# A mirrored spectrum formed by accumulating DMAs instead of extra matmuls, in a gated state-space and expert-mix kernel

## The chip, the cores and the metric

One NeuronCore of a Trainium2 chip. The time is device microseconds of one execution; the median of three runs counts. Engines: PE (matrix multiply, with PEld loading its weights), DVE (vector), ACT (scalar), POOL (GpSimd) and SP (which mostly issues DMAs).

## The reference, cut to what matters

```python
x = A_u                                              # (1, 2048, 512) bf16
g = sigmoid((x * gate_w).sum(-1, keepdims=True))
# a: K[d, l] = Re sum_n C[d,n] * exp(dt[d] * A[d,n] * l) * dt[d] * B[d,n],   l = 0..2047, n = 0..127
#    y = causal convolution of x with K along l (FFT of length 4096), a = bf16(y) + x * Dskip
# b: r = x @ w_r; the two tokens with the largest r go through a gated MLP (512 -> 1792 -> 512);
#    its result times sigmoid(r) is added to those two rows of x
return g * a + (1 - g) * b
```

## The kernel before, in words

All data lies in one SBUF tensor `AR`, cut by hand into buffers with fixed offsets; PSUM is four tensors `ps` of two banks. The convolution goes through transforms written as matmuls. The 2048 tokens are two blocks (`blk`) of 1024, the 512 channels two halves (`h`) of 256.

- `tab1` and `tab2` build the powers of the kernel's poles for one half (exponentials and sines on ACT, products on DVE; `trig` makes the sines), `kgen` multiplies the two tables on PE, `kspec` turns the result into the spectrum `KK[h]` with the constants `KP` (loaded by SP).
- `routing` transposes U into `XT`, makes the gates and the router logits, picks the two tokens and runs their MLP with the weights `WG`, `WU`, `WD`. The finished rows come by an indirect DMA on POOL (L854), and U is then read again from the output (`reload`).
- `forward(blk)` is the transform of the input U with the constants `F[ft]`, four frequency tiles `ft`. A frequency and its mirror share their work: with E the part of the even tokens and O that of the odd ones, the one is E + O (`pm` 0), the other E - O (`pm` 1). Before the change each tile issues 16 matmuls of 512 columns for E + O (two parts, real and imaginary, eight steps each), an eviction into X, 8 more matmuls with `UO`, which is the odd tokens times -2, on top of the same PSUM banks, and a second eviction (L881 are the matmuls, L466 the evictions, L472 the scaling into UO).
- `products` multiplies X with KK on DVE (L451; its big instructions are 128x4096) and forms the sum and the difference of the two mirrored halves in place in X. Its temporaries are `pqa`, `pqb`, `pqc`.
- `inverse` transforms back on PE (L1028) on top of PSUM banks that ACT has filled with the other branch (L462, 256 columns), evicts times the gate into U (L1036), and DMAs the output.

Every operation is recorded in program order with its reads and writes, and its number is its place there. Nothing is scheduled on the chip: the string `ORDER` lists the operations by number, three base-36 digits each, and each engine takes its own in that order. Operations with two forms, such as `EV` (L466, copy), `SCL` (L472, scale) or an angle addition (L650), carry both, and the digit of `SECOND` at the operation's number chooses between ACT and DVE. `PLACES` gives each PSUM bank or temporary its place. Waits are worked out from the reads and writes. DMA issues are operations too, on SP, ACT or POOL, and wait in their queue like any other. The shared line of a helper covers many operations: L451 is every `TT` on DVE, L466 every `EV`, L475 every issue of a DMA by `DMA`.

`X` holds 32 KB per partition, ordered by half, block, part and `pm`; `XT` and `WD` lie for a time where the second block of X will be.

Of the kernel before, what the change touches and what calls it, by code (L numbers as in the profile page):

```python
# [241 lines left out]
MUL1 = [(16, 4, 24, 4, 1), (20, 0, 24, 4, 1), (28, 15, 24, 4, -1)]  # L242
# [11 lines left out]
ACC = ((1, 0),)  # L254
CPE = (0,)
# [97 lines left out]
def small_mats():  # L353
# [15 lines left out]
POOLS = {"pqa": 2, "pqb": 2, "pqc": 4}  # L369
ORDER = (  # L370
    "01l00200k01501600500000u00100400700o00p00q00601j01g00t00w00v01001201h01d01901e01100900r01a00300s01701x00801v00d00g00h02701t00x01r01y01400y01300c00f00z"
    "00l02500b00i01800a02801c01s01w01p01q00n00e02302601u02101z05n02402002201b03w04002901f06i01o01n03x08d03y06h08f05m02a02j03v02k01i04102l08e01m02b06j02m03z"
    "02n02c02o00m03702p05302q02r04202d02s06k02t06l04302u03404b05402v02w04506m04405h02x04802y04902z04a04c03003804603103204p04d05503904q04f03304704g04e04i04j"
    "03c03503l03d04h05g04k05o04m04r06p03g04l04n04u06q05q03h04o06n04s03i04w06o04t05604v06w03k00j03p03o06v06y06x03m03j06r08r01k06s04y03a04z03605p05707003n06z"
    "05805b05006t05i05907107204x07307405a08i08q05r05c06u07607505108g08j08h07807705205k08s05j05z07a03q08k07905d07h07b08t05l03b08u03r05e07c05s06003s07e07f03t"
    "07g07i08l06107j07d06606508n08v06306708x08o08y05f08m08w06206806909l06a08p08z07l07k07n09009206409u09m07m07o07q07z07r09107p09409309509n07s09o09r09609p07w"
    "07u09t07t07x09q09s09z0970980800a006b06c09c0990a20a102e09a09b09d08a06d09v09w05u05t09e0a30a408909g06f09h0a60a509x09f0a70a809i0aa06e0a905v07v05w07y05x03e"
    "06g08308403f09y09k0ac0ab08109j0ad0ae0820ag08b0af08508808c03u0aq0ar0ay0860aj0as0at05y0az0ao0ap0au0ah0ai0al0ak0am0an0b00b10av0aw0ax0ch0b80b90bc0be0870bb"
    "0bi0bf02f0ba0bd0bh0ci0cj0bg0bk0c40c10bj02g0ck0bz0cl0bl0bn0bm0b50bw02h0bo0b20b60c00b30b40br0c30bx0c20by0bp0bs0bq0bt0b70ct0bu02i0c50c60c70c90e80e70e90c8"
    "0cm0cu0bv0cn0co0cr0cv0d30cs0ea0cy0cb0eg0ez0cp0d40cw0cx0cz0eb0eh0cq0d10em0ep0d00e60d50ec0d20d60f40ed0e50d70f00f50ee0f10f20f60eq0df0er0ca0cc0dg0ei0es0f9"  # L380
    "0ef0f30ce0cd0f70f80dh0dn0fw0d80fx0dc0db0d90fy0ej0cf0dl0g40da0ek0en0et0fa0cg0dp0dv0dd0eu0di0dj0dk0do0dy0fz0de0eo0fs0g00dz0e00dq0dm0ds0g10g50dr0ft0fb0fc"
    "0g20fu0fv0el0fd0fe0fg0gc0gp0ff0dw0gm0dx0gd0g60g30go0gn0ge0gq0gt0gr0dt0fh0fi0fk0fj0ey0gf0g90gx0gu0ev0gg0ga0gs0e40e30du0gb0e20ew0e10g70gi0gw0gh0ex0gv0gz"
    "0fl0gk0fm0fo0fn0gl0gy0h80h00fp0h40fq0h10fr0h20g80gj0h50h30h60h70hh0hg0hc0h90ha0hd0he0hi0hf0hb0hj"
)
SECOND = (
    "000000000000000000000000000000000000100000000000000000000000000010101000101010100000000100000000000000000000000000100010000000000000000000000001000101"
    "001110010100010010000010010010000100000000000000000000000000000000000000000000000000000000001010000010000000000001000000000000000000000000000000000000"
    "000000000101000000010100011010000010011010000000100010001000001000000000000000000000000000000000000000000000000000000000000000000000000000000000000000"
    "000000000000000000000000000000000000000000000000000000000000000000000000000000000000000000000000000000000000000000000000000000000000001000000000000000"
    "00000000000000010000001100100000"  # L390
)
PLACES = (
    "2004756176414666666067000110100264042421011602064766100101111004004220204264646600000004406600706142350206200227354163"
# [4 lines left out]
def bass_gated_mix__ssm_conv_s4__moe_arch_mod__prompt_kernel(nc, A_u, A_A_re, A_A_im, A_B_re, A_B_im, A_C_re, A_C_im, A_log_dt, A_Dskip,  # L398
# [22 lines left out]
    with ExitStack() as es:  # L421
# [42 lines left out]
        def EV(o, a, rd, wr, **k):  # L464
            n = nel(o)
            return P.op((ACT, DVE), (lambda h: h.activation(out=o, in_=a, func=ACTF.Copy), lambda h: h.tensor_copy(o, a)), rd, wr,  # L466
                        cost=(0.185 + n * 0.833e-3, 0.16 + n * (1.04e-3 if a.dtype == F32 else 0.52e-3)), **k)
        def AFF(o, a, c, d, rd, wr):
            return P.op((DVE, ACT), (lambda h: h.tensor_scalar(out=o, in0=a, scalar1=c, scalar2=d, op0=ALU.mult, op1=ALU.add), lambda h: h.activation(out=o, in_=a, func=ACTF.Copy, scale=c, bias=d)), rd, wr, cost=(0.18, 0.2))
# [24 lines left out]
        UO = B("uo", oF + 16 * KB, 4 * KB)  # L494
# [3 lines left out]
        XB = [[B("x%d%d" % (h_, k_), oX + (16 * h_ + 8 * k_) * KB, 8 * KB) for k_ in range(2)] for h_ in range(2)]  # L498
# [17 lines left out]
        XT = [B("xt%d" % i, oX + (16 * (i // 2) + 8 + 4 * (i % 2)) * KB, 4 * KB) for i in range(4)]  # L516
        WD = [B("wd%d" % i, oX + (16 * i + 8) * KB, 8 * KB) for i in range(2)]
# [5 lines left out]
        PQR = [[B("pqa", oTI[0], 8 * KB), B("pqb", oTI[0] + 8 * KB, 8 * KB)], [B("pqc", oI, 16 * KB)] * 2]  # L523
# [60 lines left out]
        for r in range(2):  # L584
            P.op(PE, scaled(at(AL, r * 512), 0, True, 1 + r), [(PRM, 0), DG], [(AL, r)], cost=0.5 * (1 + r))
        P.op(PE, scaled(at(tb_), 1, True), [(PRM, 1), DG], [tb_], cost=0.5)
# [7 lines left out]
        for i in range(2):  # L594
            P.op(PE, ptr(i), [(PRM, 2 + i), CBI], [(cc, i)], cost=0.5)
        for i in range(2):
            P.op(PE, scaled(at(bd, i * 512), 4 + i, True), [(PRM, 4 + i), DG], [(bd, i)], cost=0.5)
# [56 lines left out]
        def tab1(h, ts):  # L654
            tr = TP[h][1]
            e = lambda *ss: [(tr, ("e", s)) for s in ss]
            for o, a, b, n, d in MUL1:
                src = [a + i * d for i in range(n)]
                assert all(T1[o + i] == T1[x] + T1[b] for i, x in enumerate(src))
                v = lambda s0, st: tr(0, 128, 4 * s0, (128, 64), (st, n), (1, 4))  # L660
                TT(v(o, 4), v(a, 4 * d), v(b, 0), ALU.mult, e(b, *src), e(*range(o, o + n)))
# [32 lines left out]
        def tab2(h, ts):  # L694
# [11 lines left out]
            TT(pair(q2(0), q2(1)), pair(sq(eb, 0), sq(di, 0)), pair(sq(eb, 0), sq(di, 0)), MUL, ed, [(qa, 0), (qa, 1)])  # L706
# [32 lines left out]
        def routing():  # L739
            for q in range(8):  # L740
# [8 lines left out]
                EV(XT[0](0, 128, q * 256, (8 * KB, 2), (L, 2), (1, 256)), bb(0, 128, 0, (512, 2), (256, 2), (1, 256)), [bb], [(XT[i], q) for i in range(4)])  # L749
# [118 lines left out]
        def forward(blk):  # L868
                SCL(UO(0, 128, 0, (1, 4 * D)), U(0, 128, (blk * 8 + 1) * D, (2 * D, 4), (1, D)), -2.0, uk(*range(blk * 8 + 1, blk * 8 + 8, 2)), [UO])
                for ft in range(4):  # L870
                    pb = psum(2, full=True)
                    for pm in range(2):
                        for part in range(2):
                            def fw(h, blk=blk, ft=ft, pm=pm, pb=pb, part=part):
                                last = None
                                o = pb(0, 128, part * 512, (1, 512))
                                for par in range(pm, 2):
                                    for st in range(4):
                                        w = F[ft](0, 128, ((par * 4 + st) * 2 + part) * 128, (1, 128))
                                        x = UO(0, 128, st * D, (1, D)) if pm else U(0, 128, (blk * 8 + st * 2 + par) * D, (1, D))  # L880
                                        last = h.matmul(o, w, x, start=(pm + par + st == 0), stop=(par == 1 and st == 3), skip_group_check=(pm == 1))  # L881
                                return last
                            P.op(PE, fw, [F[ft]] + ([UO] if pm else uk(*range(blk * 8, blk * 8 + 8))), [(pb, part)], cost=(8 - 4 * pm) * 0.2157)
                        EV(X(0, 128, blk * 4096 + ft // 2 * 1024 + pm * 512 + ft % 2 * 256, (2048, 2), (8192, 2), (1, 256)), pb(0, 128, 0, (512, 2), (256, 2), (1, 256)),
                           [pb], [xk(hh, blk, part, pm, ft) for hh in range(2) for part in range(2)])
# [75 lines left out]
        def products(h, qds, blks):  # L961
# [3 lines left out]
            xo = lambda blk, part, pm: h * 8192 + blk * 4096 + part * 2048 + pm * 512 + q0  # L965
# [7 lines left out]
            tmp = lambda k: place("pq%s" % ("ab"[k] if h == 0 else "c"), PQR[h][k], (oTI[0] + 8 * k * KB, oI)[h], 8 * W, n=2)  # L973
            qk = lambda b, *ks: [(b, k) for k in ks]
            for blk in blks:
                p = tmp(0)
                TT(o2(p), x2(blk), k2(0), MUL, kx(blk) + kk(0, 0) + kk(0, 1), qk(p, 0, 1, 2, 3))
                if blk == 1:
                    t = tmp(1)
# [15 lines left out]
                else:  # L995
                    if blk == 1:
                        TT(vall(p), vall(p), vall(t), ADD, qk(t, 0, 1, 2, 3), qk(p, 0, 1, 2, 3))
                    TT(u(0), u(0), u(3), SUB, qk(p, 3), qk(p, 0))
                    TT(u(1), u(1), u(2), ADD, qk(p, 2), qk(p, 1))
                for parts in (((0,), (1,)) if last(h, blk, qds[-1]) else ((0, 1),)):  # L1000
                    n, p0 = len(parts), parts[0]
                    y = lambda pm: p(0, 128, (2 * p0 + pm) * W, (2 * W, n), (1, W))
                    for pm, op in ((0, ADD), (1, SUB)):
                        TT(X(0, 128, xo(blk, p0, pm), (2048, n), (1, W)), y(0), y(1), op, qk(p, *parts), [xk(h, blk, part, pm, ft) for part in parts for ft in fts])
        def inverse(h):
            for blk in (1, 0):
# [11 lines left out]
                for q in range(2):  # L1018
                    for t2 in range(2):
                        for par in range(2):  # L1020
                            pb = bufs[t2, par]
                            for cs in (((0, 2), (1, 3)) if last(h, blk, q) else ((0, 1, 2, 3),)):
                                def iv(hh, blk=blk, par=par, t2=t2, pb=pb, q=q, cs=cs):
                                    r = None
                                    for e in range(2):
                                        for c in cs:
                                            part, ft = c % 2, 2 * q + c // 2
                                            r = hh.matmul(pb(0, 128, e * 256, (1, 256)), G(0, 128, ((par * 2 + part) * 4 + ft) * 512 + (2 * t2 + e) * 128, (1, 128)),  # L1028
                                                          X(0, 128, h * 8192 + blk * 4096 + part * 2048 + ft // 2 * 1024 + par * 512 + ft % 2 * 256, (1, 256)), start=False, stop=(q == 1 and e == 1 and c == 3), skip_group_check=True)
# [4 lines left out]
                            for e, tb in enumerate(tbs(t2, par)):  # L1034
# [82 lines left out]
```

## Time and profile before

| what | value |
|---|---|
| runs | 153.46, 152.22, 152.40 us, median 152.40 |
| the profiled execution | 153.67 us in all, span 151.9 us |
| granted TensorE clock | 0.988 |
| busy: PE, DVE, ACT, POOL | 140.4, 140.1, 128.3, 6.7 us |
| forward matmuls L881 | 192, 44.9 us busy |
| DMA | 22.01 MB, mean 145 GB/s |

The span runs from the first to the last instruction of the profiled execution. Busy time counts instructions that overlap once; a row's mean is one instruction's own duration, which for DVE and ACT is about 0.1 us longer than its step to the next. In a timeline row the first number is the start and the second the time to the end of the last of its instructions. Windows show busy time per engine in a stretch, with the number of instructions.

### The profile page before, as it was taken

To read this page: it belongs to the slowest core of one execution; us is meant where nothing else is said; L and a number is where in the kernel's file an instruction comes from. 1 tells how busy PE (TensorE), PEld (TensorE's weight loads), DVE (VectorE), ACT (ScalarE), POOL (GpSimd) and SP (SyncE) were. 2 spreads that over 40 slices of the span, in tenths; PEclk is the share of its full clock that TensorE was granted. 3 is DMA by queue.
4 is the path that set the end of the run, shared out by engine and by line. 5 is a ranking of instruction groups with operands and counts; after the bars stand their busy time and mean duration, and the time that the engine had idled before them with its cause. 6 is when DMAs were issued, how large, how long until landed. Compare 5 with 4: busy or idle time off the path is not lost.

```text
span 151.9 us, 3913 instructions
## 1 busy us (share of the span) xinstructions
PE 140.4 (92%) x1677; PEld 101.9 (67%) x1677; DVE 140.1 (92%) x201; ACT 128.3 (84%) x215; POOL 6.7 (4%) x13
## 2 busy tenths in 40 slices
PE   1977969999999999979999999999999999999990
PEld 1866633665446447975436889987888678888980
DVE  0489999999999999988999999999999999999972
ACT  3589999999999979998996568486999899899831
POOL 3000000000000000000540000010000000000000
PEclk9999999996899999999999999999999999999999
DMA  4899999939000001600029920007920000202166
GB/s 117 287 368 413 406 405 394 349 104 539 17 0 4 0 0 27 254 4 0 0 63 296 403 76 0 4 4 218 404 76 0 0 2 4 71 0 69 39 198 182
DMA packets 12435, 22.01 MB, mean 145 GB/s; under 512 B 1111, under 2 KB 8034, under 8 KB 12258
## 3 DMA queue, kind: packets, MB, share of 16 engines
q1 hardware_dynamic: 11410, 21.11, 39.4%
q10 hardware_dynamic: 976, 0.66, 1.5%
q8 instruction: 13, 0.21, 0.6%
q14 instruction: 4, 0.03, 0.1%
q0 software_dynamic: 32, 0.00, 0.1%
HBM read 19.66 MB, written 4.20 MB: 157 GB/s over the span
## 4 chain that ended last, share of the span: by engine, by line
PE 76%; DVE 13%; ACT 6%; issue 1%; DMA 1%; SPq 0%; DVEq 0%
PE ps L881 22%; PE ps L1028 18%; PE ps L954 12%; PE ps L899 8%; DVE AR L451 5%; ACT AR L466 3%; DVE AR L466 3%; PE ps L912 3%; PE ps L990 2%; PE ps L829 2%; PE ps L580 2%; ACT AR L462 2%; DMA AR<-c_bf 1%; PE ps L591 1%; DVE AR L472 1%
## 5 line engine op out<-in xcount | busy, mean ns | idle before, releaser
L451 DVE TENSOR_TENSOR AR<-AR 128x1024 bf16<-128x1024 bf16 (+8 forms) x132 | 118.5, 949 | 5.5 <-ACT AR L462 3.7
L466 ACT ACTIVATE AR<-ps 128x1024 bf16<-128x1024 f32 (+10 forms) x60 | 49.6, 861 | 11.3 <-PE ps L954 3.9
L881 PE MATMUL ps<-AR 128*128 128x512 bf16 x192 | 44.9, 389 | 0.0
L881 PEld LDWEIGHTS ps<-AR 128*128 128x128 bf16 x192 | 18.5, 100 | 21.8 <-issue 1.6
L1028 PE MATMUL ps<-AR 128*128 128x256 bf16 x256 | 29.3, 273 | 0.0
L1028 PEld LDWEIGHTS ps<-AR 128*128 128x128 bf16 x256 | 24.9, 98 | 3.5 <-DVE AR L451 0.3
L954 PE MATMUL ps<-AR 128*128 128x256 bf16 x160 | 19.0, 273 | 0.0
L899 PE MATMUL ps<-AR 128*128 128x84 bf16 (+1 forms) x512 | 18.0, 196 | 0.9 <-ACT AR L462 0.9
L899 PEld LDWEIGHTS ps<-AR 128*128 128x128 bf16 x512 | 17.9, 96 | 1.3 <-issue 1.0
L462 ACT ACTIVATE AR<-AR 128x1024 bf16<-128x1024 int16 (+5 forms) x24 | 18.2, 772 | 0.5 <-DVE AR L451 0.3
L462 ACT ACTIVATE ps<-AR 128x256 f32<-128x256 bf16 (+1 forms) x36 | 18.0, 545 | 0.1
L954 PEld LDWEIGHTS ps<-AR 128*128 128x128 bf16 x160 | 15.5, 98 | 2.9 <-DMA AR<-c_ksp 0.2
L1036 ACT ACTIVATE AR<-ps,AR 128x256 bf16<-128x256 f32 x27 | 11.8, 480 | 4.3 <-PE ps L1028 3.4
L472 ACT ACTIVATE AR<-AR 128x256 int32<-128x256 f32 (+3 forms) x30 | 14.7, 528 | 0.2 <-DVE AR L451 0.2
L462 ACT ACTIVATE AR<-ps 128x512 bf16<-128x512 f32 (+1 forms) x18 | 12.4, 773 | 2.3 <-PE ps L580 2.3
L650 ACT ACTIVATE AR<-AR 128x1024 int32<-128x1024 int32 (+1 forms) x9 | 8.2, 912 | 0.0
L472 DVE TENSOR_SCALAR AR<-AR 128x1024 bf16<-128x1024 bf16 (+3 forms) x20 | 7.3, 368 | 0.1
L591 PE MATMUL ps<-AR 128*128 128x128 bf16 x8 | 2.2, 488 | 3.4 <-DMA AR<-c_bf 3.4
L746 PE MATMUL ps<-AR 128*128 128x128 bf16 x64 | 4.3, 220 | 0.9 <-DVE AR L466 0.9
L580 PE MATMUL ps<-AR 128*128 128x128 bf16 x24 | 4.6, 414 | 0.2 <-DMA AR<-in_A_A_im_dram 0.2
L746 PEld LDWEIGHTS ps<-AR 128*128 128x128 bf16 x64 | 3.7, 99 | 1.3 <-DVE AR L466 1.1
L580 PEld LDWEIGHTS ps<-AR 128*128 128x128 bf16 x24 | 3.8, 183 | 1.0 <-DMA AR<-in_A_A_im_dram 0.5
(63 smaller groups left out, 81.7 us busy)
## 6 DMA issues: line engine op xcount, KB each, us to landing
AR<-c_ksp SPq DMA_DIRECT2D x5, 512.0 KB, 4.4
AR<-in_A_u_dram SPq DMA_DIRECT2D x4, 512.0 KB, 7.4
AR<-c_fwd SPq DMA_DIRECT2D x4, 512.0 KB, 8.8
AR<-out_dram SPq DMA_DIRECT2D x4, 512.0 KB, 7.0
AR<-c_inv SPq DMA_DIRECT2D x1, 2048.0 KB, 7.7
AR<-in_B_w_up_dram SPq DMA_DIRECT2D x1, 1792.0 KB, 13.3
AR<-in_B_w_gate_dram SPq DMA_DIRECT2D x1, 1792.0 KB, 18.1
out_dram<-AR SPq DMA_DIRECT2D x14, 128.0 KB, 2.2
```

The lines of the kernel that those rows point to most:

```text
L451: return P.op(DVE, lambda h: h.tensor_tensor(out=o, in0=a, in1=b, op=op), rd, wr, cost=cst or tt_cost(o, a, b), **k)
L462: return P.op(ACT, lambda h: h.activation(out=o, in_=a, func=func, scale=scale, bias=bias), rd, wr, cost=0.185 + nel(o) * 0.833e-3 + (0.09 ...
L466: return P.op((ACT, DVE), (lambda h: h.activation(out=o, in_=a, func=ACTF.Copy), lambda h: h.tensor_copy(o, a)), rd, wr, cost=(0.185 + n * ...
L472: return P.op((ACT, DVE), (lambda h: h.activation(out=o, in_=a, func=ACTF.Copy, scale=c), lambda h: h.tensor_scalar(out=o, in0=a, scalar1= ...
L580: last = h.matmul(o, PRM(0, 128, i * D + k * 128, (1, 128)), DG(0, 128, k * 128, (1, 128)), start=(r + k == 0), stop=(r == reps - 1 and k ...
L650: P.op((DVE, ACT), (lambda hh: hh.tensor_scalar(out=w, in0=w, scalar1=16384.0, scalar2=None, op0=ALU.add), lambda hh: hh.activation(out=w, ...
L746: last = h.transpose(bb(0, 128, db * 256 + t_ * 128, (1, 128)), U(0, 128, (2 * q + t_) * D + db * 128, (1, 128)), IDN(0, (1, 128)))
L881: last = h.matmul(o, w, x, start=(pm + par + st == 0), stop=(par == 1 and st == 3), skip_group_check=(pm == 1))
L899: last = hh.matmul(pb(0, 128, g // 6 * 512 + g % 6 * W4 + o, (1, n)), TP[h][1 - i // 2](0, 128, (b0 + g) * 128, (1, 128)), r[i](0, 128, (b ...
L954: last = hh.matmul(pb(0, 128, n * 256, (1, 256)), KP[u](0, 128, tau * 128, (1, 128)), KC[h](0, 128, jg * 256, (1, 256)), start=(k == 0 and ...
L1028: r = hh.matmul(pb(0, 128, e * 256, (1, 256)), G(0, 128, ((par * 2 + part) * 4 + ft) * 512 + (2 * t2 + e) * 128, (1, 128)), X(0, 128, h * ...
L1036: P.op((ACT, DVE), (lambda hh, o=o, i_=i_, g_=g_: hh.activation(out=o, in_=i_, func=ACTF.Copy, scale=g_), lambda hh, o=o, i_=i_, g_=g_: hh ...
```

## The change

- `forward`: for each tile, 8 matmuls of the even tokens are evicted times -2 into the place of the mirror, then 8 matmuls of the odd tokens are added on the same banks and evicted as they are. After every second tile a DMA on POOL's queue adds the full sum to the place of the mirror (`accum_op`): E + O - 2E = O - E. UO is gone. In `products` sum and difference change places, since the mirror has the other sign.
- X is ordered by block, half, part and `pm`, so that one such DMA covers both halves and parts: four DMAs of 512 KB. XT and WD lie together in block 1.
- Squares may go to ACT (`SQ`): one product of `tab1` in each half is now a square, and the square in `tab2` may be on either engine.
- In `inverse`, two evictions become one operation, except in the last block; on ACT it still issues two activations.
- Temporaries of the products have four pools (`pqa`, `pqb` one place each, `pqc`, `pqd` two each) in other regions.
- `ORDER`, `SECOND` and `PLACES` are new throughout. The accumulating DMAs stand in POOL's queue behind the memset of `snc112`, in the order blk 1 half 1, blk 1 half 0, blk 0 half 0, blk 0 half 1, ahead of the memset of `OHR`. On DVE the first products are those of X blk 1 with the first part of KK and X blk 0 with the second, for both halves of the frequencies of `h` 0. On SP a reload of part of U stands among the loads of KP, whose last is the one over F0.
- Costs in `cost=` are the planner's and change nothing on the chip; `DAC` is empty.

```diff
-MUL1 = [(16, 4, 24, 4, 1), (20, 0, 24, 4, 1), (28, 15, 24, 4, -1)]
+MUL1 = [(16, 4, 24, 4, 1), (20, 0, 24, 4, 1), (28, 7, None, 4, -1)]
...
+        def SQ(o, a, rd, wr):
+            n = nel(o)
+            return P.op((DVE, ACT), (lambda h: h.tensor_tensor(out=o, in0=a, in1=a, op=ALU.mult), lambda h: h.activation(out=o, in_=a, func=ACTF.Square)), rd, wr,
+                        cost=(0.157 + n * 0.52e-3, 0.185 + n * 0.833e-3))
...
-        UO = B("uo", oF + 16 * KB, 4 * KB)
...
-        XB = [[B("x%d%d" % (h_, k_), oX + (16 * h_ + 8 * k_) * KB, 8 * KB) for k_ in range(2)] for h_ in range(2)]
+        XB = [[B("x%d%d" % (h_, k_), oX + (16 * k_ + 8 * h_) * KB, 8 * KB) for k_ in range(2)] for h_ in range(2)]
...
+        PQO = {"a": (oTI[0],), "b": (oTI[0] + 8 * KB,), "c": (oI, oI + 8 * KB), "d": (oR + 24 * KB, oTI[1])}
...
-            TT(pair(q2(0), q2(1)), pair(sq(eb, 0), sq(di, 0)), pair(sq(eb, 0), sq(di, 0)), MUL, ed, [(qa, 0), (qa, 1)])
+            SQ(pair(q2(0), q2(1)), pair(sq(eb, 0), sq(di, 0)), ed, [(qa, 0), (qa, 1)])
...
         def forward(blk):
-                SCL(UO(0, 128, 0, (1, 4 * D)), U(0, 128, (blk * 8 + 1) * D, (2 * D, 4), (1, D)), -2.0, uk(*range(blk * 8 + 1, blk * 8 + 8, 2)), [UO])
                 for ft in range(4):
                     pb = psum(2, full=True)
-                    for pm in range(2):
+                    for par in range(2):
                         for part in range(2):
...
-                                for par in range(pm, 2):
-                                    for st in range(4):
...
-                        EV(X(0, 128, blk * 4096 + ft // 2 * 1024 + pm * 512 + ft % 2 * 256, (2048, 2), (8192, 2), (1, 256)), pb(0, 128, 0, (512, 2), (256, 2), (1, 256)),
-                           [pb], [xk(hh, blk, part, pm, ft) for hh in range(2) for part in range(2)])
+                                for st in range(4):
+                                    last = h.matmul(pb(0, 128, part * 512, (1, 512)), F[ft](0, 128, ((par * 4 + st) * 2 + part) * 128, (1, 128)), U(0, 128, (blk * 8 + st * 2 + par) * D, (1, D)),
+                                                    start=(par + st == 0), stop=(st == 3), skip_group_check=(par == 1))
+                                return last
+                            P.op(PE, fw, [F[ft]] + uk(*range(blk * 8 + par, blk * 8 + 8, 2)), [(pb, part)], cost=4 * 0.2157)
+                        o, i_, sc = X(0, 128, blk * 8192 + ft // 2 * 1024 + (1 - par) * 512 + ft % 2 * 256, (2048, 2), (4096, 2), (1, 256)), pb(0, 128, 0, (512, 2), (256, 2), (1, 256)), (-2.0, 1.0)[par]
+                        P.op((ACT, DVE), (lambda hh, o=o, i_=i_, sc=sc: hh.activation(out=o, in_=i_, func=ACTF.Copy, scale=sc), lambda hh, o=o, i_=i_, sc=sc: hh.tensor_scalar(out=o, in0=i_, scalar1=sc, scalar2=None, op0=ALU.mult)),
+                             [pb], [xk(hh, blk, part, 1 - par, ft) for hh in range(2) for part in range(2)], cost=(0.185 + 1024 * 0.833e-3, 0.16 + 1024 * 1.04e-3))
+                    if ft % 2:
+                        xv = lambda pm: X(0, 128, blk * 8192 + ft // 2 * 1024 + pm * 512, (2048, 4), (1, 512))
+                        xs_ = lambda pm: [xk(hh, blk, part, pm, f) for hh in range(2) for part in range(2) for f in (ft - 1, ft)]
+                        P.op(POOL, lambda hh, d=xv(1), c=xv(0): hh.dma_start(d, c, accum_op=ADD), xs_(0), xs_(1), cost=1.3, nbytes=524288, dma=True, tag="acc")
...
-                    for pm, op in ((0, ADD), (1, SUB)):
+                    for pm, op in ((0, SUB), (1, ADD)):
...
-                            for e, tb in enumerate(tbs(t2, par)):
-                                o, i_, g_ = U(0, 128, tb * D + h * HC, (1, HC)), pb(0, 128, e * 256, (1, HC)), SG(0, 128, 64 + tb, (1, 1))
+                            tb0 = tbs(t2, par)[0]
+                            for ee in (((0,), (1,)) if last(h, blk, q) else ((0, 1),)):
```

109 lines of the change are left out of this document (65 added, 44 removed).

## The prediction

> **What bounds the kernel now.** First the shares of the engines. No engine stands out: PE, DVE and ACT are all near full.
>
> ```profile
> span 151.9 us, 3913 instructions
> ...
> PE 140.4 (92%) x1677; PEld 101.9 (67%) x1677; DVE 140.1 (92%) x201; ACT 128.3 (84%) x215; POOL 6.7 (4%) x13
> ...
> PE 76%; DVE 13%; ACT 6%; issue 1%; DMA 1%; SPq 0%; DVEq 0%
> PE ps L881 22%; PE ps L1028 18%; PE ps L954 12%; PE ps L899 8%; DVE AR L451 5%; ACT AR L466 3%; DVE AR L466 3%; PE ps L912 3%; PE ps L990 2%; PE ps L829 2%; PE ps L580 2%; ACT AR L462 2%; DMA AR<-c_bf 1%; PE ps L591 1%; DVE AR L472 1%
> ```
>
> The chain that ended last runs 76% over PE, and its largest line is the forward transform (L881). Whoever stops here expects the whole of a cut in L881. So the next view is the stages, by windows (columns: PE, PEld, DVE, ACT, POOL busy).
>
> ```profile
> 8.00:13.00 5.00, 4.19 (x55) 3.55 (x53) 4.87 (x7) 4.50 (x8) 0.31 (x1) 1.00 1.02 393
> 13.00:64.00 51.00, 48.45 (x621) 28.45 (x622) 50.97 (x97) 49.37 (x83) 0.31 (x1) 0.97 0.56 203
> 64.00:70.00 6.00, 5.07 (x119) 4.33 (x116) 4.67 (x9) 5.36 (x12) 0.00 (x0) 1.00 0.02 5
> 70.00:146.00 76.00, 75.97 (x854) 59.77 (x852) 75.39 (x85) 63.21 (x106) 4.64 (x3) 1.00 0.27 91
> 146.00:152.00 6.00, 2.15 (x20) 1.67 (x18) 2.27 (x5) 1.86 (x4) 0.00 (x0) 0.96 0.64 184
> ```
>
> DVE works 50.97 us of 51 and 75.39 of 76. From 8.1 to 146 us its only visible gap is 1.23 us:
>
> ```profile
> 68.97 0.69 DVE L451 TENSOR_TENSOR AR<-AR 128x1024 bf16<-128x1024 bf16 x1 [1.23 <-PE ps L899]
> ```
>
> So PE and DVE are two chains of equal length, and the chain view shows only one of them. Work taken off PE alone cannot move the end: DVE's 140.1 us, its late start (6.2 us idle before 8.1) and a tail after its last product remain. What leaves DVE is what counts. ACT is as full as DVE up to 64 us (49.37 of 51), so it cannot take much from DVE there.
>
> **The change part by part.**
>
> PE, forward transform: before, each of 8 blocks (2 row blocks, 4 frequency tiles) issues 16 matmuls for the sum and 8 more with UO; after, 8 and 8. That removes 64 of 192. The chain counts 48 of them as 10.51 us, 0.219 each, so PE loses 64 x 0.219 = 14.0 us. On the end this is worth 0: DVE covers it. Were DVE free, it would be worth up to 14.
>
> The two UO scalings go: one on DVE (0.61 from its start at 22.27 to the next at 22.88), one on ACT.
>
> ```profile
> L472 ACT ACTIVATE AR<-AR 128x2048 bf16<-128x2048 bf16 x1 | 1.9, 1910 | 0.0
> ...
> L472 DVE TENSOR_SCALAR AR<-AR 128x2048 bf16<-128x2048 bf16 x1 | 0.7, 686 | 0.0
> ...
> L650 DVE TENSOR_SCALAR AR<-AR 128x512 int32<-128x512 int32 x1 | 0.4, 419 | 0.0
> ```
>
> The 16 evictions keep shape and engine (ACT, 1.02 each); a scale of -2 in an activation is bounded by 0 and by the difference between scaled and plain forms, L462 256-wide 0.48 against L1036 0.48, so 0. The swap of ADD and SUB in products is the same instruction: 0.
>
> Engine choices: I numbered the operations in program order and compared SECOND digit by digit, with the time from one start to the next, since a row's duration overlaps its neighbour by about 0.08 us. DVE loses UO 0.61; one transposed-input eviction net (two leave, one comes) 0.60; four 128x1024 negations 4 x 0.33; one 128x1024 square in tab2 0.60; one 128x512 angle addition 0.33. It gains one 128x1024 addition (no such row; between the 0.33 of 128x512 and twice that; I take 0.60), five 128x256 angle scalings net 5 x 0.20, and some small routing copies 0.25. Sum: -3.46 + 1.85 = **-1.6 us**. ACT takes the opposite and loses 1.81 of UO: net +2.1 us, nearly all before 80 us. All 12 merged output evictions are on ACT, where one operation still issues two activations: 0. DVE keeps five single output evictions: 0. The count of DVE operations stays 201.
>
> Accumulating DMAs: four of 512 KB on POOL's queue. There POOL issues them behind the memset of snc112, which waits for a DVE operation some 70 us in, and in the order blk 1 half 1, blk 1 half 0, blk 0 half 0, blk 0 half 1; behind them only the OHR memset. They can only go after the last forward evictions, which ACT's new order puts about where its 120th operation ends now, at 78 to 80 us. When are they needed? The first products now are, in order, X blk 1, X blk 0 (half 0), X blk 1, X blk 0 (half 1). The first 128x4096 product starts at 92.1 now; by DVE's new order the work ahead of it is 0.9 us shorter: 91.2, then 93.4, 95.6, 97.8 at 2.2 apart. No row shows such a DMA. The nearest:
>
> ```profile
> AR<-c_ksp SPq DMA_DIRECT2D x5, 512.0 KB, 4.4
> AR<-in_A_u_dram SPq DMA_DIRECT2D x4, 512.0 KB, 7.4
> ...
> AR<-c_inv SPq DMA_DIRECT2D x1, 2048.0 KB, 7.7
> ...
> out_dram<-AR POOLq DMA_INDIRECT x1, 5.8
> ```
>
> From below: c_inv moves 2 MB in 7.7, 1.9 per 512 KB; with three accesses (read, read, write) for two, 2.9. From above: 7.4, the 512 KB loads of the crowded start. With t per DMA, one after the other from 80 us, the second lands at 80+2t, the third 80+3t, the fourth 80+4t; all are in time up to t = 4.4 us. I take 2.9 to 4.4, nearest to c_ksp, whose loads run in the same stretch: hidden behind DVE's table work up to 91 us, so 0 us, with a margin of 0 to 6 us. POOL's own time (4 issues of 3.81 at most) is free: it is busy 6.7 us of the span. Above 4.4 it costs up to 4 us per us of t.
>
> [...] The row: POOL's one software DMA took 3.81 us to issue 2 KB while DVE was busy 2.00 of 2.00, and DVE's neighbours kept their usual 0.28 and 0.41. [...] What a starved issue would cost is worked out as a rival below.
>
> SP's queue: its K-spectrum loads now sit behind one reload of U, and the last waits for F0. By ACT's sums F0 is free near 76 us, against 79.4 now; 4.4 us to land gives 80 to 82, and now the first L954 starts at 83.9. So it is early by 2 to 3 us, which an accumulating DMA beside it could eat: 0.
>
> New pq places ("c", "d", two each) only take waits away: 0. kgen's start follows DVE (prefix 48.0 us of work now against 51.3): 3.3 us earlier, no price.
>
> The tail: DVE's last X write ends at 145.96 now, then 16 matmuls (1.75), then evictions to 149.18. After, the last five DVE evictions follow the last groups more evenly: last group at +1.75, two evictions of 0.48: +2.7 against +3.2. Worth -0.4.
>
> Sum: 151.9 - 1.6 - 0.4 = 149.9 in the profiled span, if DVE has as little idle as now. That execution lasted 153.67 in all; the runs have a median of 152.4, so the -2.0 is taken from it: **150.4 us**.
>
> **The rivals.**
>
> 1. Two waits of DVE on PE go too, since PE has 14 us to spare: the gap of 1.23 and the 0.55 us before its line at 8.13 (for L580), 150.4 - 1.8 = 148.6. For it: the one DVE gap waits on L899 (PE) at 66 to 68 us. Against: the wait ahead of L899 was for ACT (0.93 us, L462), and ACT gets fuller.
>
> 2. The new order gives the gain back in small DVE waits. By the sums of ACT and DVE, DVE reaches the trig results (snc100, snc101, snc211) within 0.5 us of ACT finishing them, three or four times: +0.5 each, 152.0. For it: both engines full up to 64 us. Against: the present order has the same tightness and loses 1.2 us.
>
> 3. Slower: the accumulating DMAs are late, at DVE's first products. At t = 5.8 (the POOL row) the third lands at 97.4 against 93.4, +4.0, the fourth at 103.2 against 101.8, +1.4: 155.8. At t = 7.4 the second is 3.6 late, the third another 5.2, the fourth another 3.0: 162.2. Middle 159. It decides from t = 4.4. [...] Against: the DMA engines are nearly idle from 88 to 102 us now (shares of 0.09 and less).
>
> 4. Starved issue: POOL issues nothing while DVE runs product after product and only goes on when DVE stalls at 91.2; four issues of 3.81 and 2.0 to land (5.8 - 3.8), less three products of 2.2: +10.6, 161. For it: in this trace POOL issues nothing in the stretch of the products, so nothing shows it can. Against: that issue of 3.81 us went through amid a full DVE. [...]
>
> 5. The order opens larger DVE gaps elsewhere (late KP, a PSUM bank held): 155.
>
> **How the numbers follow.** Forecast 150.4, its own range 149.4 to 151.4: 0.48, of which 0.34 is below 150.9. Rival 1: 0.12. Rival 2: 0.14. Rival 3: 0.13. Rival 4: 0.04. Rival 5: 0.09. One per cent (150.9 and 153.9) is about what a measurement of this kernel can tell from no change. Faster 0.34 + 0.12 = 0.46; within 1% 0.14 + 0.14 = 0.28; slower 0.26. The range goes from 148.4 (rival 1) to 156.5, which holds rival 5 and the lower end of rival 3 and leaves out rival 4 and the upper part of 3.
>
> **What would show it.** Right: L881 x128; PE busy near 126 with gaps, DVE near 138.5 and still the dense engine up to its last product at about 144; ACT near 130; no DVE wait on a DMA at the first 128x4096 product. Wrong: DVE idle before the products with the accumulating DMA as releaser (3, 4), POOL issues much over 3.8 us, DVE waits on ACT's L462 adding up to over 2 us (2), PE still full.

## The result, and the profile after

The changed kernel takes 153.93 us (median of 20 runs, 153.35 to 155.92) against 152.91 for the kernel before on the same chip (20 runs): ratio 1.0071, 95% interval 1.0048 to 1.0093. On another chip the same two kernels came to 153.79 (12 runs) and 153.75 (22 runs), ratio 1.001 (0.998 to 1.004). So the change costs something between nothing and 0.9%. The forecast was a gain of 1.3%. In the experiments below the runs of the kernel before differ with the granted clock, 46 at 0.995 or more with a median of 153.24 us and 45 at 0.989 or less with 154.31; whether that makes the difference between the two chips is not shown.

The page after, first the shares and the chain that ended last:

```profile
span 152.3 us, 3796 instructions
...
PE 129.2 (85%) x1613; PEld 95.0 (62%) x1613; DVE 138.4 (91%) x201; ACT 130.1 (85%) x213; POOL 25.5 (17%) x17
...
PE 56%; DVE 22%; ACT 8%; DMA 5%; issue 4%; SPq 3%
PE ps L1052 18%; DVE AR L452 14%; PE ps L975 12%; PE ps L920 11%; DMA AR<-in_A_u_dram 5%; PE ps L933 3%; SPq L480 3%; ACT AR L463 3%; PE ps L1010 2%; PE ps L849 2%; ACT AR L901 2%; DVE AR L456 1%; PE ps L896 1%; ACT AR L467 1%; PE ps L828 1%
...
L896 PE MATMUL ps<-AR 128*128 128x512 bf16 x128 | 32.2, 399 | 5.0 <-ACT AR L901 4.9
```

The work went where the prediction sent it: 64 forward matmuls fewer (L896, 128), DVE 1.7 us less, ACT 1.8 us more. The forward line, 22% of the chain before, is down to 1%. And the span is 0.4 us longer. The windows (columns PE, PEld, DVE, ACT, POOL) say in which stage the gain was lost:

```profile
8.00:13.00 5.00, 3.51 (x52) 2.79 (x50) 5.00 (x8) 5.00 (x8) 0.31 (x1) 1.00 1.04 385
13.00:64.00 51.00, 40.91 (x584) 24.14 (x582) 48.03 (x97) 47.64 (x78) 17.89 (x3) 0.87 0.54 194
64.00:70.00 6.00, 6.00 (x114) 4.38 (x110) 5.61 (x13) 5.63 (x9) 0.00 (x0) 1.00 0.30 90
70.00:146.00 76.00, 71.68 (x829) 57.56 (x829) 75.18 (x80) 66.40 (x112) 6.06 (x6) 1.00 0.46 121
```

DVE's idle time between 13 and 64 us was 0.03 and is now 2.97. From 8 to 146 us in all it was 2.10 (138.0 less 135.90) and is 4.18 (138.0 less 133.82): +2.08. Less work of 1.7 against more idle time of 2.1 is the 0.4 us by which the span grew. The timeline of DVE (start, length, and in brackets the idle time before it) has the gap by name:

```profile
14.10 1.29 DVE L467 COPY AR<-ps 128x1024 bf16<-128x1024 bf16 x2 [0.46 <-PE ps L766]
32.40 1.89 DVE L452 TENSOR_TENSOR AR<-AR 128x512 bf16<-128x512 bf16 x3 [2.26 <-PE ps L849]
67.52 0.69 DVE L452 TENSOR_TENSOR AR<-AR 128x1024 bf16<-128x1024 bf16 x1 [0.32 <-PE ps L920]
96.10 12.30 DVE L452 TENSOR_TENSOR AR<-AR 128x4096 bf16<-128x4096 bf16 x7 [0.45 <-ACT AR L467]
```

One wait of 2.26 us at 30.1 is as long as the whole loss; the small ones stand against a gap of 1.23 that is now 0.32. DVE waits for PE's L849, the gate and up matmuls of the expert MLP, since a table product of `tab2` that the new order puts there writes over WG and WU. Why was PE late? The timeline of PE, with two DMA issues of SP that follow:

```profile
24.85 1.76 PE L828 MATMUL ps<-AR 128*128 128x2 bf16 x64
26.88 2.75 PE L849 MATMUL ps<-AR 128*128 128x2 bf16 x98 [0.27 <-ACT AR L467]
30.35 0.67 SPq L480 DMA_DIRECT2D out_dram<-in_A_u_dram  x1
31.06 0.57 SPq L480 DMA_DIRECT2D AR<-c_fwd  x1
31.84 0.51 PE L849 MATMUL ps<-AR 128*128 128x2 bf16 x14 [2.21 <-issue]
```

PE stops after 98 of 112 small matmuls, in the middle of one operation of 56, where the program has no wait, and goes on 2.21 us later with the last 14. "issue" is the profile's word for idle time that nothing it shows explains. In the views of the DMA queues the stretch 20 to 29 us has no packet on the queue named instruction, and 29 to 30.3 has one:

```profile
q1 hardware_dynamic: 188, 0.33, 70.5%
q8 instruction: 1, 0.02, 5.0%
```

In the trace this packet of 16384 bytes starts at 29.22 and ends at 30.25 us; the one before started at 17.14. The first of the two copies to the output, which the trace shows in the same hole, is issued at 30.35, after PE had stopped.

### The profile page after: what moved, and what is told of

Same layout as the page of the kernel before. It is cut to its first block, busy times and chain, and to the rows that moved or that the text cites. A ratio compares the mean times of both kernels' runs of the same rounds, so it can differ in the third digit from the quotient of the medians.

```text
span 152.3 us, 3796 instructions
## 1 busy us (share of the span) xinstructions
PE 129.2 (85%) x1613; PEld 95.0 (62%) x1613; DVE 138.4 (91%) x201; ACT 130.1 (85%) x213; POOL 25.5 (17%) x17
## 4 chain that ended last, share of the span: by engine, by line
PE 56%; DVE 22%; ACT 8%; DMA 5%; issue 4%; SPq 3%
PE ps L1052 18%; DVE AR L452 14%; PE ps L975 12%; PE ps L920 11%; DMA AR<-in_A_u_dram 5%; PE ps L933 3%; SPq L480 3%; ACT AR L463 3%; PE ps L1010 2%; PE ps L849 2%; ACT AR L901 2%; DVE AR L456 1%; PE ps L896 1%; ACT AR L467 1%; PE ps L828 1%
## 5 line engine op out<-in xcount | busy, mean ns | idle before, releaser
L452 DVE TENSOR_TENSOR AR<-AR 128x1024 bf16<-128x1024 bf16 (+7 forms) x128 | 115.2, 959 | 7.1 <-ACT AR L463 3.7
L467 ACT ACTIVATE AR<-ps 128x1024 bf16<-128x1024 f32 (+9 forms) x43 | 34.8, 845 | 6.9 <-PE ps L975 3.1
L896 PE MATMUL ps<-AR 128*128 128x512 bf16 x128 | 32.2, 399 | 5.0 <-ACT AR L901 4.9
L1052 PEld LDWEIGHTS ps<-AR 128*128 128x128 bf16 x256 | 24.9, 98 | 3.4 <-DVE AR L452 0.3
L896 PEld LDWEIGHTS ps<-AR 128*128 128x128 bf16 x128 | 12.2, 103 | 21.0 <-ACT AR L901 7.7
L920 PE MATMUL ps<-AR 128*128 128x84 bf16 (+1 forms) x512 | 18.1, 196 | 0.6 <-issue 0.4
L920 PEld LDWEIGHTS ps<-AR 128*128 128x128 bf16 x512 | 17.8, 96 | 1.4 <-issue 1.2
L975 PEld LDWEIGHTS ps<-AR 128*128 128x128 bf16 x160 | 15.4, 98 | 3.3 <-DVE AR L452 0.3
L874 POOL DMA_INDIRECT out_dram<-AR x1 | 17.3, 17327 | 0.6 <-ACT AR L474 0.6
L901 ACT ACTIVATE AR<-ps 128x1024 bf16<-128x1024 f32 x16 | 16.0, 1005 | 0.0
L477 ACT ACTIVATE AR<-AR 128x256 int32<-128x256 f32 (+2 forms) x28 | 14.8, 554 | 0.0
L906 POOL DMA_DIRECT2D AR<-AR x4 | 5.2, 1713 | 6.7 <-ACT AR L477 5.4
L477 DVE TENSOR_SCALAR AR<-AR 128x256 int32<-128x256 f32 (+2 forms) x20 | 5.9, 322 | 0.0
L766 PE MATMUL ps<-AR 128*128 128x128 bf16 x64 | 4.4, 219 | 1.7 <-DMA AR<-in_A_u_dram 1.6
## 6 DMA issues: line engine op xcount, KB each, us to landing
AR<-AR POOLq DMA_DIRECT2D x4, 512.0 KB, 12.7
```

Source lines behind the costliest of these rows:

```text
L452: return P.op(DVE, lambda h: h.tensor_tensor(out=o, in0=a, in1=b, op=op), rd, wr, cost=cst or tt_cost(o, a, b), **k)
L874: P.op(POOL, lambda h: h.indirect_dma_start(dr(out, 0, (D, L), (1, D)), bass.IndirectOffsetOnAxis(ap=IDX(0, 2, 0, (1, 1)), axis=0), ZB(0, ...
L896: last = h.matmul(pb(0, 128, part * 512, (1, 512)), F[ft](0, 128, ((par * 4 + st) * 2 + part) * 128, (1, 128)), U(0, 128, (blk * 8 + st * ...
L901: P.op((ACT, DVE), (lambda hh, o=o, i_=i_, sc=sc: hh.activation(out=o, in_=i_, func=ACTF.Copy, scale=sc), lambda hh, o=o, i_=i_, sc=sc: hh ...
L920: last = hh.matmul(pb(0, 128, g // 6 * 512 + g % 6 * W4 + o, (1, n)), TP[h][1 - i // 2](0, 128, (b0 + g) * 128, (1, 128)), r[i](0, 128, (b ...
L975: last = hh.matmul(pb(0, 128, n * 256, (1, 256)), KP[u](0, 128, tau * 128, (1, 128)), KC[h](0, 128, jg * 256, (1, 256)), start=(k == 0 and ...
```

## The experiments

Theory A: PE had used up its instructions and waited for the next block of them; the border is the place in PE's stream of instructions where one block ends and the next begins. Theory B: it waited for something that the matmuls read or share. Ratios are to the kernel before on the same chip, with 95% intervals. The first four kernels ran on one chip, the next three on a second, the two after them on a third and the last on a fourth.

**The block's border moved, one step, and PE's time taken away by itself.** In the first two, extra matmuls stand ahead of the forward tiles (shown) and of one of the transposed tables (`PADT`):

```diff
+PAD, PADT = {(0, 3, 0, 0): 18, (0, 3, 0, 1): 24, (0, 2, 0, 1): 8}, 14
...
                             def fw(h, blk=blk, ft=ft, par=par, pb=pb, part=part):
                                 last = None
+                                for _ in range(PAD.get((blk, ft, par, part), 0)):
+                                    h.matmul(pb(0, 128, part * 512, (1, 2)), F[ft](0, 128, part * 128, (1, 128)), U(0, 128, blk * 8 * D, (1, 2)), start=True, stop=True)
```

> The changed kernel with 64 extra two-column matmuls on PE ahead of 24 us (14 in the transposed tables, 50 in three forward tiles of blk 0, into banks that the next matmul starts anew). Theory A, instructions: in the trace of the changed kernel PE stops at 29.63 us in the middle of the gate and up matmuls (L849), and the only packet of the instruction queue between 18 and 39 us goes from 29.22 to 30.25; PE waits for its next block of instructions. A packet is 16384 bytes, 256 instructions of 64 bytes, and a matmul with its weights is two; 64 extra pairs bring the block's border 128 instructions forward, ahead of the 64 + 112 pairs that run without a pause. So the stop of 2.21 goes, DVE's wait of 2.26 with it, and the time is 153.9 - 2.2 = 151.7. Theory B, data or clock: PE stops for something that the matmuls read or share (DMAs that crowd, the copies from DRAM to DRAM, the halved clock); extra matmuls on PE change nothing of that: stop still there, 153.9 or up to 1 us more.

Measured: ratio 0.9889 (0.9836 to 0.9942), median 152.14. The stop is gone; the same 112 matmuls run through, and DVE doesn't wait for them.

```profile
26.38 1.76 PE L831 MATMUL ps<-AR 128*128 128x2 bf16 x64
28.40 3.13 PE L852 MATMUL ps<-AR 128*128 128x2 bf16 x112 [0.27 <-ACT AR L468]
```

The kernel with 64 more matmuls on PE is faster than the one without, by 1.2% (0.9889 against 1.001) or 1.8% (against 1.007); theory A expected 1.4% (2.2 of 153.9). The packet that had started at 29.22 starts at 23.88. The extra matmuls cost DVE 1.3 us of new waits for the routing's transposes (L803), so the stop's whole price is more than the difference of the medians.

With twice as many:

```diff
+PAD, PADT = {(0, 2, 0, 0): 10, (0, 3, 0, 0): 32, (0, 3, 0, 1): 36, (0, 2, 0, 1): 26}, 24
```

> The same with 128 extra matmuls, 256 instructions, which is one whole block: the border comes back to where it was against the gate and up matmuls. Theory A: the stop of about 2.2 us in L849 is there again, with an instruction packet at its start and end, and the time is 153.9 or somewhat over it (PE has 3.5 us more to do between 14 and 24 us, of which some 1.7 lay in its gaps). Theory B: as with 64, whatever that showed. A third possibility, C, that any delay of the gate and up matmuls cures the stop: then it is gone here as well, 151.7 to 152.7.

Measured: 1.0131 (1.0073 to 1.0189). The time looks like theory A's, but for another reason: L852 runs through in one piece, and what costs is 2.9 us of DVE waits for L803 behind the many extra matmuls. Theory A's expectation for the stop is a miss. The border alone doesn't make it. One block earlier, among the extra matmuls, this kernel has a stop that the kernel with 64 has not. It ends 1.55 us after an instruction packet ended (at 18.33):

```profile
19.87 0.48 PE L899 MATMUL ps<-AR 128*128 128x2 bf16 x12 [0.63 <-issue]
```

The operation moved on PE, in `ORDER` (number 223 ahead of 126):

```diff
-L849 Matmult ps<-AR 128x2 x112
+L849 Matmult ps<-AR 128x2 x56
 L896 Matmult ps<-AR 128x512 x4
+L849 Matmult ps<-AR 128x2 x56
```

> The changed kernel with one operation moved on PE: four forward matmuls (blk 1, tile 2, even tokens, imaginary part) now stand between the gate and the up matmuls instead of behind them, as forward matmuls stood there before the change. Theory A: the block comes when it comes; PE does 0.9 us of other work in front of the stop, the stop shrinks to about 1.3, the last 14 up matmuls still end near 32.3, and DVE still waits for them: 153.9, at most 0.3 less. Rival D, that PE only can't take 112 pairs of small matmuls in a row, and a pause of a microsecond lets it catch up: no stop, the up matmuls end at about 31, time 152.6.

Measured: 1.0008 (0.9974 to 1.0042), and in the trace:

```profile
26.90 1.57 PE L849 MATMUL ps<-AR 128*128 128x2 bf16 x56 [0.27 <-ACT AR L467]
28.33 1.87 PE L896 MATMUL ps<-AR 128*128 128x512 bf16 x4
29.99 1.20 PE L849 MATMUL ps<-AR 128*128 128x2 bf16 x38
31.52 0.62 PE L849 MATMUL ps<-AR 128*128 128x2 bf16 x18 [0.33 <-issue]
```

Four matmuls went ahead, and 18 instead of 14 were left at the stop. Counted from the start (matmuls, weight loads and the records of PE's sequencer), PE stops ahead of its 706th recorded instruction in both kernels; the stop of 0.63 us with 128 extra matmuls stands ahead of the 450th, which is 256 earlier. So a place in the instruction stream decides, not the length of the row of small matmuls (rival D falls), and DVE still waits 2.0 us.

Last, the kernel before with PE's work cut and nothing else:

```diff
                                         x = UO(0, 128, st * D, (1, D)) if pm else U(0, 128, (blk * 8 + st * 2 + par) * D, (1, D))
+                                        if pm:
+                                            o, x = pb(0, 128, part * 512, (1, 2)), UO(0, 128, st * D, (1, 2))
```

> The kernel before the change with its 64 UO matmuls cut from 512 columns to 2 (so the mirrored part is formed in two columns only); the number of instructions is kept. PE loses 64 x (0.219 - 0.027) = 12.3 us, its busy time goes from 140.4 to about 128, and nothing else changes. If DVE sets the end, as the prediction says, this is worth 0, or up to 1.2 if DVE's one visible wait for PE (1.23 us at 68.97) goes: 151.2 to 152.9 beside 152.4 to 152.9. If PE's chain sets it, as the chain of waits alone would suggest (L881 22%), it is worth several us: 141 to 148.

Measured: 1.0009 (0.997 to 1.0048).

```profile
PE 131.7 (86%) x1677; PEld 100.6 (66%) x1677; DVE 140.0 (92%) x201; ACT 128.5 (84%) x215; POOL 6.7 (4%) x13
```

PE loses 8.7 us of busy time and the kernel nothing that its interval of 0.4% lets one see. (Not 12.3: the granted clock fell from 0.988 to 0.943, and other matmuls took longer, those of L899 before, for instance, 20.0 us in all against 17.9.) DVE's gap ahead of kgen's selection did not go: it is 1.84 us here against 1.23, and the profile now names ACT as the one that ended it. That the forward line held 22% of the chain of waits told nothing of its worth.

**Border and crowd.** What the second run left open is answered by the delay of the packet. Call a stretch in which the DMA engines are full of loads a crowd. The stops ahead of the 450th and the 706th record are 256 records apart. With that as the length of a block, PE enters it 256 records ahead of its border, and the delay in the table is the time from there to the start of the next packet:

| kernel, block | entered | packet starts | delay | packet's end + 1.55 | block used up |
|---|---|---|---|---|---|
| before | 28.9 | 31.08 | 2.2 | 33.7 | 34.5 |
| after | 25.7 | 29.22 | 3.5 | 31.8 | 29.6, stop to 31.84 |
| one operation moved | 25.7 | 28.93 | 3.2 | 31.5 | 31.2, stop to 31.52 |
| 64 extra, first | 21.4 | 23.88 | 2.5 | 26.6 | 29.3 |
| 64 extra, second | 29.3 | 29.70 | 0.4 | 32.5 | 37.2 |
| 128 extra, first | 19.9 | 23.53 | 3.7 | 26.2 | 29.0 |
| 128 extra, second | 29.0 | 29.65 | 0.7 | 32.3 | 32.6 |

1.55 us is the time from the packet's end to PE's next instruction in the stops (1.59 and 1.56 here). After the change the DMA engines are full to about 29 us with WU, WG, w_down and constants (mean shares of 1.02 to 1.13 from 20 us on, then 0.83; before it to 31, with 1.02 to 1.10, then 0.44); the blocks of the table entered in that time wait 2.2 to 3.7 us for their packet, those entered at its end less than 1. Theory A2: a stop needs both, a block that PE uses up in about 4 us, as rows of small matmuls do, and a request in the crowd. Two kernels take from the crowd and leave PE's stream as it is.

```diff
-                DMA([(WD[i](0, 128, 0, (D, n), (1, D)), dr(B_w_down, f0 * 128 * D, (D, 128), (128 * D, n), (1, D)))], [], [WD[i]], n * 131072)
+                DMA([(WD[i](0, 128, 0, (D, 1), (1, D)), dr(B_w_down, f0 * 128 * D, (D, 128), (128 * D, 1), (1, D)))], [], [WD[i]], n * 131072)
```

> The changed kernel with 2 of the 14 row groups of w_down loaded instead of 14 (1.57 MB less; the two expert rows come out with other numbers), nothing else moved. What the last runs left open is why the extra matmuls cured the stop even where the block's border came back to its old place. Theory A2, border and crowd together: PE enters the block at about 25.8 us, runs through its 128 small pairs in 3.9 us, and the request for the next one waits in DMA engines that are full until 29 us (delays from entry to packet: 1.9 to 4.8 us for nine blocks entered in the crowd, 0.3 and 0.65 for the two entered at 29 us). 1.57 MB at 355 GB/s is 4.4 us: the crowd ends near 24.6, the packet starts by 26.5, the stop of 2.2 us and DVE's wait of 2.26 go, 153.9 - 2.2 = 151.7. Theory E, that only the place of the border or the time at which the gate and up matmuls begin matters (both are unchanged here): the stop stays and so does the time, 153.9.

Measured: 0.992 (0.9879 to 0.9961), median 151.89, span 150.0. The packet starts at 26.89, the stop is gone. The windows 26 to 27 us of this kernel and of the changed one, whose last two columns are the mean share of the DMA engines and GB/s:

```profile
26.00:27.00 1.00, 1.00 (x46) 1.00 (x43) 1.00 (x2) 1.00 (x5) 0.00 (x0) 1.00 0.26 93
```

```profile
26.00:27.00 1.00, 0.73 (x30) 0.64 (x27) 1.00 (x1) 0.88 (x5) 0.00 (x0) 1.00 1.11 350
```

The first window has a quarter of the load of the second. PE's instructions are the same and the block is entered 0.6 us later (26.3), but the packet needs 0.6 us instead of 3.5. So theory E falls: the crowd is the second condition.

```diff
 L480 DMACopy AR<-in_B_w_down_dram 128x8x512
-L480 DMACopy AR<-c_fwd 128x2048
-L480 DMACopy AR<-c_bf 128x544
 L480 DMACopy out_dram<-in_A_u_dram 16x32768
-L480 DMACopy AR<-c_fwd 128x2048
+L480 DMACopy AR<-c_fwd 128x2048 x2
 L480 DMACopy out_dram<-in_A_u_dram 16x32768
+L480 DMACopy AR<-c_bf 128x544
```

> The changed kernel with two loads on SP moved back: F1 (512 KB) behind the first of the two copies of the input to the output, the second part of c_bf behind the second. The whole reference is computed. Theory A2: 0.65 MB leave the crowd, 1.8 us at 355 GB/s; the engines run dry near 27.3 while the first copy waits for w_down to land; the packet that started at 29.22 starts near 27.5, and of the stop of 2.2 us some 0.4 or nothing is left: 151.7 to 152.1. Against it: F1 may come late for the tile that needs it (38 to 40 us), which PE can bear and DVE doesn't see. Theory E: the stop stays, 153.9.

Measured: 0.9989 (0.9942 to 1.0035). The crowd ended only near 28, the packet started at 28.32, and a stop of 1.55 us was left: the right direction, 0.66 us of the 1.8 expected. I had taken the loads as one line that gets shorter; the page doesn't show which transfer would fill the room.

**The accumulating DMAs made small.** On the kernel with 64 extra matmuls:

```diff
-                        xv = lambda pm: X(0, 128, blk * 8192 + ft // 2 * 1024 + pm * 512, (2048, 4), (1, 512))
+                        xv = lambda pm: X(0, 128, blk * 8192 + ft // 2 * 1024 + pm * 512, (2048, 4), (1, 8))
```

> The kernel with 64 extra small matmuls (no stop; ratio to before 0.989), and the four accumulating DMAs cut from 512 columns to 8 (the mirrored part is then right in few columns only): 32 KB instead of 2 MB in all. If they are hidden, as the prediction has it, the time stays within 0.3 us of that kernel's, ratio 0.987 to 0.991. If their 12.7 us in flight, among the loads of the constants and of U, cost DVE, ACT or PE something that no wait names, it falls, by up to 1.5 us: 0.979.

Measured: 0.9907 (0.9862 to 0.9952) against 0.9889: no gain that the intervals show. They are hidden, span 149.8.

**Versions of the whole reference without the stop.** w_down is loaded later, behind F1 and c_bf on SP, and waits for XS:

```diff
-... [], [WD[i]], n * 131072)
+... [XS], [WD[i]], n * 131072)
```

> The changed kernel with the two loads of w_down (1.79 MB) moved behind F1 and the second part of c_bf on SP, and made to wait for the gathered tokens (XS, written by ACT just before the gate matmuls start). The whole reference is computed; no instruction is added. Theory A2: without w_down the DMA engines run dry near 25 us, the packet of instructions goes out by 27, the stop of 2.2 us is gone; w_down is then asked for at 26.9 and takes 5.1 us at 355 GB/s plus some 2, 34, where the down matmuls start now at 34.4 to 36.8, so nothing is late: profiled span 150.0 as in the run with less of w_down, ratio to before 0.987 to 0.993. Against it: a late w_down holds up the copies and the down matmuls, and DVE's write of the finished rows behind them, +1 us; or the stop only moves to the next block: no gain, 1.007.

> The changed kernel itself once more, on the same chip as the run beside it, so that the two can be set against the same runs of the kernel before. Expected: ratio 1.005 to 1.009, an instruction packet between 28 and 31 us, a stop of PE about 2 us long in L849 with 14 matmuls left, and DVE waiting as long.

Measured side by side: 0.9915 (0.9883 to 0.9946) with w_down later, median 152.79, and 1.001 (0.9979 to 1.004), 153.79, for the changed kernel as it is, which shows its stop of 2.01 us with 14 left. With w_down later the block is entered at 26.2, and from 26.2 to 27.7 us two packets in all are on the queues:

```profile
q8 instruction: 1, 0.02, 4.3%
q1 hardware_dynamic: 1, 0.00, 0.0%
```

```profile
27.31 3.13 PE L849 MATMUL ps<-AR 128*128 128x2 bf16 x112 [0.27 <-ACT AR L467]
```

The packet starts at 26.63 and no stop follows. Part of the gain goes again, as the expectation had it: w_down's result reaches DVE late (view of waits: us in total, times, longest):

```profile
DVE AR L456 <- PE ps L870: 1.0, 1, 1.0
```

The last run puts one long table product of DVE ahead of the instruction that waits (in `ORDER`, number 266 ahead of 137):

```diff
+L452 TensorTensor AR<-AR 128x3584
 L456 TensorScalarPtr AR<-ps,AR 2x512
-L452 TensorTensor AR<-AR 128x3584 x2
+L452 TensorTensor AR<-AR 128x3584
```

> The run with w_down later (ratio 0.9915) showed no stop, but a new wait of DVE, 0.96 us at 41.8 for the transposed result of the down matmuls (L870), which came 1 us later than before. Here one 128x3584 product of DVE's tables (1.7 us) goes ahead of the instruction that waits; nothing else is changed and the whole reference is computed. If that wait is all that the late load costs, the span falls from 151.5 to 150.5 and the ratio to about 0.985; if the rows are then late for POOL's indirect DMA, the reload of U and the rest behind it, it stays at 0.9915.

Measured: the wait is gone and the profiled span is 150.5, as expected; the ratio is 0.9966 (0.993 to 1.0002), not 0.985. Its interval meets that of the run before (0.993 to 0.9946), so whether the last edit brings anything isn't settled. For the cause this run is the cleanest of all. Up to the stop PE keeps the times of the changed kernel (the block entered at 25.72 in both, L849 started at 26.88 in both), but the packet starts at 26.05 instead of 29.22:

```profile
26.88 3.14 PE L849 MATMUL ps<-AR 128*128 128x2 bf16 x112 [0.27 <-ACT AR L467]
```

So rival C (any delay of these matmuls cures the stop) falls as well. Two versions that compute the whole reference beat both kernels: 64 extra matmuls (0.9889) and the later w_down (0.9915).

## Why the prediction was wrong

- **The sum for DVE was right.** DVE 140.1 to 138.4 (forecast -1.6), ACT 130.1 (forecast near 130), the count of instructions 201. Without the stop the span is 150.0 (less w_down), 149.8 (small accumulates) and 150.5 (last run); the forecast was 149.9. The first two compute less than the whole reference. In two more kernels without the stop another wait of DVE stood in: 151.2 with 64 extra matmuls (1.3 us for L803) and 151.5 with w_down later (1.0 for L870).
- **PE's 14 us are worth 0: shown**, within 0.4%, by the cut in the kernel before, 1.0009. PE's busy time fell by 11.2 instead of 14; the granted clock fell too, from 0.988 to 0.955.
- **The step that failed** is the condition on the sum, "if DVE has as little idle as now". The edit on PE was costed in microseconds at nothing, and its instructions were not looked at as a supply that comes in packets (12 of 16384 bytes on the instruction queue after the change). Before, eight and then four forward matmuls of 512 columns stood between the gathering, the gate and the up matmuls, so that PE used up its block in 5.6 us (28.9 to 34.5), and by the table (33.7 against 34.5) the next was there 0.8 us early. After, 64 + 112 pairs of small matmuls stand in a row and 3.9 us used up the block. The order did a second thing: the block is entered 3.2 us earlier, deeper in the crowd, and its packet starts 3.5 us after the entry instead of 2.2. Even 5.6 us would then have been too short by 0.5 (25.7 + 5.6 = 31.3 against 31.8, an estimate from the table); the run with one operation moved, 31.2 against 31.5, bears it out. The first view to look at would have been PE's order around L829, with the page's row for the instruction queue beside the DMA share of 1.0.
- **Rival 2** (small DVE waits, for ACT's trig results) named about the right amount and the wrong place: DVE waited 0.45 us once where the profile names ACT, and 2.26 once for PE. **Rival 5** (gaps elsewhere) was the right kind; its price, 4.6 us over the forecast, was twice the wait of 2.26.
- **Rival 1** came about in its own two waits and not in its time: the gap of 1.23 before kgen's selection is 0.32 now and the 0.55 before 8.13 is gone, but 0.46 at 14.10 is new, and the 2.26 outweighs both.
- **Accumulating DMAs, hidden at 2.9 to 4.4 us each**: right in sum, with no margin. (The three accesses for two behind the 2.9 were the author's estimate; no view shows them.) In the page they take 12.7 us each from issue to landing:

```profile
q0 software_dynamic: 2144, 2.10, 9.2%
...
AR<-AR POOLq DMA_DIRECT2D x4, 512.0 KB, 12.7
```

  They run side by side from 80.6 to 98.4 us; their packets take 13.9 us on all 16 engines, 3.5 per DMA. In the first profile of the changed kernel no wait of DVE bears their name, but the third lands at 95.98, inside the gap of 0.45 us before the second 128x4096 product (96.10); the profile names ACT, whose eviction came 0.08 us later still. In three others DVE waits for them by name, 0.2 to 0.7 us. With 128 extra matmuls:

```profile
97.19 4.49 DVE L453 TENSOR_TENSOR AR<-AR 128x4096 bf16<-128x4096 bf16 x2 [0.67 <-DMA AR<-AR]
```

  The forecast's margin of 0 to 6 us was 0: from 79 to 97 us they held 75.5% of the 16 engines, and reloads of U and the other loads 35.1% beside them. (The accumulating DMAs lie on queue q0 and those loads on q1: what they share is the engines.)
- **Rival 4**, a starved issue, did not come: POOL issued the four in 1.35 and 3.88 us, while DVE ran `TENSOR_TENSOR` without a gap (74.94 to 85.05). **The tail** brought about 0 instead of -0.4 (its own numbers, 2.7 against 3.2, give -0.5): DVE's last write to X ends 0.31 later (146.27), the last eviction 0.24 later (149.42). **The first 128x4096 product** came at 93.4 instead of 91.2: the wait of 2.26.

## What to carry to other kernels

Take work off an engine that isn't the bound and you still move its instructions: look for rows of short instructions that the long ones had kept apart, and for full DMA engines beside them, since the instructions came as DMA packets too (12 of 16384 bytes in the changed kernel), the one before the stop 3.5 us after PE had entered its block, with the engines full (mean shares of 1.08 to 1.13 from 24 to 29 us). Here an idle time put down to "issue" in the middle of an operation, with a packet on the instruction queue that ended 1.4 to 1.6 us before it did, was that stop each time. It was cured by loading less or later in the crowd (w_down), or by extra matmuls that moved the block's border.

## What the runs showed of the hardware that was not expected

**Instruction blocks.** Each packet of the instruction queue is 16384 bytes and takes 0.9 to 1.4 us in the two kernels; in the stops among two-column matmuls PE goes on 1.55 to 1.59 us after its end. 12 packets came for 3252 recorded instructions of PE (its sequencer's included), 13 for 3377. The places 256 records apart, counted on from the 450th and the 706th and back to the 194th, are as many: 12 in 3252 records, 13 in 3377. That makes 256 records to a packet and 64 bytes to a record, an estimate from these figures, with which the expectation for 64 extra matmuls had counted. The crossing of a border cost up to 2.2 us where the block before it was used up in 3.9. The rows need not be two columns wide. The changed kernel stops once more, 6 x 256 records after the first time, in L920 (68 and 84 columns), whose block was used up in 4.6 us (94.6 to 99.2) while the accumulating DMAs still ran. The packet ended at 98.23; DVE was busy and did not wait for this stop:

```profile
99.62 2.96 PE L920 MATMUL ps<-AR 128*128 128x68 bf16 x81 [0.40 <-issue]
```

In the kernel before, the 0.93 us ahead of L899 at 66.31, which the profile and the prediction put down to ACT, also stand at such a place (3 x 256 records after the 706th) and end 1.26 us after a packet; whether they were a stop too is not shown.

**The granted clock.** In the two profiles the granted clock was 0.5 from 27.2 to 40.8 us after the change, against 35.4 to 38.8 before.

**POOL's indirect DMA.** Its issue took 3.81 us before and 17.33 after, with the same bytes, and 1.53 in the last run, where it starts 1.6 us later (before, after, last run):

```profile
73.99 3.81 POOL L854 DMA_INDIRECT out_dram<-AR  x1 [0.21 <-issue]
```

```profile
L874 POOL DMA_INDIRECT out_dram<-AR x1 | 17.3, 17327 | 0.6 <-ACT AR L474 0.6
```

```profile
47.72 1.53 POOL L874 DMA_INDIRECT out_dram<-AR  x1 [3.20 <-ACT AR L477]
```

In all three DVE is busy meanwhile, mostly with products of bf16 (4.7 us of the 5.0 in its lines before, 17.2 of 19.0 after, all 2.3 in the last run). What decides is open; no wait in the profile of the changed kernel names it or the reloads of U behind it.
